# Attention, a mixture of experts and a SoLU layer in one kernel: the tiles of results moved to the front of the freed memory, and expert 1's weights issued ahead of its rows

## The chip, the cores and the metric

The kernel runs on one core of a Trainium2 chip. The metric is the device time of one execution in microseconds (us). A core has five engines with a queue of instructions each: PE (matrix products), DVE and ACT (element by element), POOL, and SP, which here only issues DMA transfers. Each queue runs in its own order, and an instruction that waits holds up all that stand behind it in its queue. A wait is a wait on counters: every engine raises a counter of its own as its instructions end, every DMA queue likewise.

## The reference

```
scores = q @ k^T / 8, times gamma_h**(i-j) for i >= j        # 4 x 8 heads x 576 x 64
x      = (scores @ v) as 2304 rows of 512
e_i    = argmax(x_i @ w_gate);  gate_i = softmax(...)[e_i]    # 8 experts, capacity 576
y_i    = gate_i * (relu(x_i @ w1[e_i]) @ w2[e_i])             # 512 -> 1024 -> 512
h      = y @ w_in;  s = h * softmax(h);  out = layernorm(s) * g @ w_out
```

## The kernel before

Attention runs over 20 chunks of 128 rows, its instructions in an order written out by hand (PERIOD, and DRAIN for the end). Each chunk's rows of x are scattered by expert into a table `xs` in DRAM (L524). Every fp32 operand is split into a high and a low fp16 part, and a product takes three matmuls.

Expert 0's first 192 rows are computed inside attention's last part (steps `el`, `ehm`, `eym`), into `eyh` and `eyl`. DRAIN ends with `cp`, the function `places`: nine small DVE instructions whose last is `offi` (L604), the places where each expert's results go.

Then `expert(e)` runs for e = 0 to 7 in the order of their loads. It takes its rows from `xs` by a transposing DMA into `xT` (`x_load`, 144 rows for what is left of expert 0, 352 for expert 1), makes four hidden pairs (fp = 0 to 3, PE L256 to L258 into `hps`), each read out by ACT (`hh`, L262) and DVE (`hl`, L266), and two output pairs (dp = 0, 1, PE L280 to L282 into `yps`), which ACT and DVE write into the tiles of results `y_hi` and `y_lo` (L286, L290). `hps` and `yps` turn through three buffers of PSUM, so a pair can start when the pair three before it has been read out.

An expert's weights come in eight parts of 512 KB, each loaded by SP into one of four `stage` buffers (`wst`, L204 and L208), split by ACT (`wh`, L178) and then by DVE (`wl`, L181). `w_step` does DVE's half of one part, issues the next load, and then ACT's half of a later part. Parts 1 to 8 are expert 0's and are loaded and split in attention; parts 9 to 16 are expert 1's (9 to 12 for hidden pairs 0 to 3, 13 to 16 for the outputs), and 17 on are expert 2's.

POOL clears the unused part of `y_hi` and `y_lo` (L1110), copies the early results in (L1107, L1108), and writes zeros into rows of `xs` that no token filled (`blank_rows`, L948). `blank_rows(NUT)` and `blank_rows(0)` stand before `x_load(1)`, which reads such rows, and behind `x_load(0)`, which reads the same table.

Memory of a core's partitions is handed out in pools, one behind the other. Attention has the pools `attn` and, behind it, `at_one`; when both are closed, the later pools are laid over them. Bytes in a partition, as the built program places them:

| pool | before | after |
|---|---|---|
| attn (freed) | 90336 to 180864 | the same |
| at_one (freed) | 180864 to 209824 | the same |
| ybuf (y_hi, y_lo) | | 90336 to 130272 |
| f64p (f64raw) | 90336 to 98528 | 130272 to 138464 |
| f3 | 98528 to 114912 | 138464 to 154848 |
| wk (xT, hh, hl, th) | 114912 to 151520 | 154848 to 191456 |
| big | 151520 to 224224 (y_hi, y_lo at its start) | 191456 to 224224 |

Of the kernel before, what the change touches and what calls it, by code (L numbers as in the profile page):

```python
# [10 lines left out]
F32 = mybir.dt.float32  # L11
F16 = mybir.dt.float16
# [8 lines left out]
N = B * S  # L21
DM = H * D
E = 8
# [8 lines left out]
COLS = (336, 352, 328, 312, 304, 296, 288, 280)  # L32

EARLY = 192
# [12 lines left out]
def rows16(n):  # L47

    return -(-n // 16) * 16
# [63 lines left out]
def tile_attention_moe_solu(ctx: ExitStack, tc: tile.TileContext, a: dict, cols, cols16):  # L113
    nc = tc.nc
    act, dve, pool, pe, sp = nc.scalar, nc.vector, nc.gpsimd, nc.tensor, nc.sync
# [97 lines left out]
    def w_load(e, h, part):  # L213
        if e not in number:
            number[e] = sp.value_load(order[0:1, e:e + 1], min_val=1, max_val=E - 1)
        wraw[e, h, part] = w_raw(number[e], h, part)
# [15 lines left out]
    def w_load_next():  # L232
        if nload[0] < len(wsteps):
            w_load(*wsteps[nload[0]])
            nload[0] += 1

    def w_hi_next(limit):
        if nhi[0] < min(limit, len(wsteps)):
            split_hi(*w_parts(*wsteps[nhi[0]]))
            nhi[0] += 1  # L240

    def w_lo_next():

        if nconv[0] < nhi[0]:
            split_lo(*w_parts(*wsteps[nconv[0]]))
            wraw.pop(wsteps[nconv[0]])
            nconv[0] += 1
            return True
# [12 lines left out]
    def hidden_hi(ps, hid, fp, n):  # L261
        act.activation(hid[0][:, 2 * fp:2 * fp + 2, :n], ps[:, :, :n], AF.Relu)  # L262
# [26 lines left out]
    def y_out_lo(ps, n, dst_lo, th):  # L289
        dve.tensor_tensor(dst_lo, ps[:, :, :n], th[:, :, :n], op=ALU.subtract)  # L290
# [237 lines left out]
    early = {}  # L528
# [230 lines left out]
    ps_pools[:] = [psA, psC, psA]  # L759


    f64p = ctx.enter_context(tc.tile_pool(name="f64p", bufs=1))
    f64raw = f64p.tile([128, 2, 512, 2], I32, name="f64raw")
    f3 = ctx.enter_context(tc.tile_pool(name="f3", bufs=2))
    wk = ctx.enter_context(tc.tile_pool(name="wk", bufs=2))
    big = ctx.enter_context(tc.tile_pool(name="big", bufs=1))
    fin = ctx.enter_context(tc.tile_pool(name="fin", bufs=1))
    s3 = ctx.enter_context(tc.tile_pool(name="s3", bufs=5))
    CMAX = max(COLS)
    LAST = [min(N, sum(COLS[:e])) for e in range(E)]  # L770
    YW = max([N] + [n + c for n, c in zip(LAST, COLS)])
    y_hi = big.tile([128, 4, YW], F16, name="y_hi")
    y_lo = big.tile([128, 4, YW], F16, name="y_lo")
    w_in_hi = big.tile([128, 4, F], F16, name="w_in_hi")
    w_in_lo = big.tile([128, 4, F], F16, name="w_in_lo")
    w_out_hi = big.tile([128, 8, DM], F16, name="w_out_hi")
# [168 lines left out]
    def blank_rows(t):  # L945

        n, u = ((E - 1) * (UNIT - 1), 1) if t == NUT else (min(128, (E - 1) * NUNIT - 128 * t), UNIT)
        pool.indirect_dma_start(out=xs_by[NCH + t].rearrange("(u r) w -> u (r w)", r=u),  # L948
                                out_offset=bass.IndirectOffsetOnAxis(ap=blank[0:n, t:t + 1], axis=0),
                                in_=f64raw[:n].rearrange("p i f t -> p (i f t)").bitcast(F16)[:, 0:u * 2 * DM], in_offset=None,  # L950
                                bounds_check=E * NR // u - 1, oob_is_err=False)

    def x_load(e):
        if e:
            n = rows16(COLS[e])
            rows = xs[:].rearrange("(e n) w -> e n w", e=E)[bass.ds(number[e], 1), 0:n, :].rearrange("e n w -> (e n) w")
        else:
            n = COLS[0] - EARLY
            rows = xs[bass.ds(sp.value_load(starti[0:1, 0:1], min_val=0, max_val=EARLY), n), :]
        xT[e] = wk.tile([128, 8, n], F16, tag="xT", name="xT")  # L960
        sp.dma_start_transpose(out=xT[e], in_=rows)
# [20 lines left out]
    def w_step(limit):  # L982

        if w_lo_next():
            w_load_next()
        w_hi_next(limit)
# [13 lines left out]
    def expert(e):  # L1000
        w = [wsplit.pop((e, 0)), wsplit.pop((e, 1)), None, None]
        C = COLS[e] if e else COLS[0] - EARLY
        hid = (wk.tile([128, 8, CMAX], F16, tag="hh", name="hh"), wk.tile([128, 8, CMAX], F16, tag="hl", name="hl"))
        for fp in range(4):
            ps = hidden_mm(w, xT[e], fp, C)
            if e or fp:
                w_step(8 * e + 12)
            hidden_hi(ps, hid, fp, C)
            hidden_lo(ps, hid, fp, C)
            f64_step(e, fp)  # L1010
            if e:
                next(side, None)
            if fp == min(e, 1) and e + 1 < E:
                x_load(e + 1)
                if not e:
                    for t in range(1, NUT):
                        blank_rows(t)
                if not e:
                    w_load_next()
        w[2], w[3] = wsplit.pop((e, 2)), wsplit.pop((e, 3))  # L1020
        at, top = (offi[0:1, e:e + 1], LAST[e]) if e else (starti[0:1, 0:1], EARLY)
        ra = act.value_load(at, min_val=0, max_val=top)
        rv = dve.value_load(at, min_val=0, max_val=top)
        for dp in range(2):
            ps = y_mm(w, hid, dp, C)
            if e:
                for _ in range(2):
                    w_step(8 * e + 16)
            th = wk.tile([128, 2, CMAX], F16, tag="th", name="th")
            y_out_hi(ps, C, y_hi[:, 2 * dp:2 * dp + 2, bass.ds(ra, C)], th)  # L1030
            y_out_lo(ps, C, y_lo[:, 2 * dp:2 * dp + 2, bass.ds(rv, C)], th)
            f64_step(e, 4 + dp)
            if not e:
                for _ in range(2):
                    w_step(8 * e + 16)


    sol = {}
# [59 lines left out]

    inorder = ExitStack()
    inorder.enter_context(tc.manual_schedule())  # L1100
    x_load(0)
    pool.memset(f64raw, 0)
    blank_rows(NUT)
    blank_rows(0)
    for _ in range(3):
        w_load_next()
    pool.tensor_copy(y_hi[:, :, 0:EARLY], early["y"][0])  # L1107
    pool.tensor_copy(y_lo[:, :, 0:EARLY], early["y"][1])  # L1108
    for t in (y_hi, y_lo):
        pool.memset(t[:, :, COLS[0]:N].bitcast(F32), 0.0)  # L1110
    for e in range(E):
        if e == 1:
            f64_next(0)
# [6 lines left out]
    for j in range(NT):  # L1120
        c = slice(128 * j, 128 * j + 128)
# [14 lines left out]
    with tc.For_i(0, nany, 1):  # L1136
        nblk = nc.values_load(bcnt[0:1, 0:1], min_val=0, max_val=NBLK)
        with tc.For_i(0, nblk, 1) as i:
            row = sp.value_load(brow[0:1, bass.ds(i, 1)], min_val=0, max_val=E * NR - 128)
            ex = sp.value_load(bexp[0:1, bass.ds(i, 1)], min_val=0, max_val=E - 1)  # L1140
            xb = wk.tile([128, 8, CMAX], F16, tag="xT", name="xb")
            w = []
# [22 lines left out]
            for h in range(4):  # L1165
                hi = wpool.tile([128, 2048], F16, tag="wh", name="whb")
                lo = wpool.tile([128, 2048], F16, tag="wl", name="wlb")
                for part in range(2):
                    t = w_raw(ex, h, part)
                    cs = slice(1024 * part, 1024 * part + 1024)  # L1170
                    split_weights(hi[:, cs], lo[:, cs], t, WS)
                w.append((hi, lo))
            hid = (wk.tile([128, 8, CMAX], F16, tag="hh", name="hhb"), wk.tile([128, 8, CMAX], F16, tag="hl", name="hlb"))
            for fp in range(4):
                hidden_pair(w, xb, hid, fp, 128)
            for dp in range(2):
                y_pair(w, hid, dp, 128, y_hi[:, 2 * dp:2 * dp + 2, 0:128], y_lo[:, 2 * dp:2 * dp + 2, 0:128],
                       wk.tile([128, 2, CMAX], F16, tag="th", name="th"))
            M_in("b", y_hi[:, :, 0:128], y_lo[:, :, 0:128], mb[:, 0:1])
# [6 lines left out]
        with tc.For_i(0, ndrop, 1):  # L1186

            for ch in range(NCH):
                b, c = divmod(ch, CPB)
                n = csize(ch)  # L1190
# [43 lines left out]
```

## Time and profile before

| | us |
|---|---|
| median of 3 runs | 529.32 (529.21 to 531.28) |
| the profiled execution | 529.27 |
| its span, first to last instruction | 527.4 |
| what lies around the span | 1.87 |

| engine | busy us | share |
|---|---|---|
| PE | 504.9 | 96% |
| DVE | 348.3 | 66% |
| ACT | 278.9 | 53% |
| POOL | 150.8 | 29% |

Attention is over for PE at 135 us, expert 0 runs to 147, expert 1 to 176, the other experts to 324, the SoLU layer to the end. PE's busy time counts overlapping matmuls once, and a matmul's row lasts longer than the distance to the next one, so the starts of the matmuls tell more than their durations.

### The profile page before, as it was taken

The page shows a single profiled execution, that of the slowest core. Times are in us where ns is not written, and L with a number is a line of the kernel's source. Part 1 is how long each engine was busy: PE and PEld are TensorE (multiplying, and loading weights), DVE is VectorE, ACT ScalarE, POOL GpSimd, SP SyncE. Part 2 cuts the span into 40 slices and gives each one's busy share as a digit, 9 for nine tenths or more (in the row PEclk, how much of TensorE's full clock was granted, in tenths as well). Part 3 has the DMA queues.
Part 4 walks back from the last instruction along what each step waited for, and adds up shares of the span by engine and source line. Part 5 has one row for each costly group of instructions (what it writes and reads, how often), then busy time and mean ns, then how long its engine had stood idle before and what let it go on. Part 6 is the DMA issues. An engine that isn't in the chain of part 4 may idle for free.

```text
span 527.4 us, 11770 instructions
## 1 busy us (share of the span) xinstructions
PE 504.9 (96%) x4616; PEld 341.2 (65%) x4616; DVE 348.3 (66%) x839; ACT 278.9 (53%) x452; POOL 150.8 (29%) x183
## 2 busy tenths in 40 slices
PE   8889999999998999999999998999999999999992
PEld 4779999989975677777777786444444444444440
DVE  0478778878657796969889994386565555556520
ACT  4688888873445646465657661264434433443430
POOL 3638687844650000202010000022221231131130
PEclk9999999999999999999999999999999999999997
DMA  8999998222689796968798830037234333333431
GB/s 214 228 248 247 256 284 208 103 62 91 177 265 281 239 257 225 250 212 253 259 238 274 219 121 0 1 64 116 60 81 93 68 80 82 79 76 71 94 81 44
DMA packets 139485, 83.09 MB, mean 158 GB/s; under 512 B 100053, under 2 KB 126581, under 8 KB 139389
## 3 DMA queue, kind: packets, MB, share of 16 engines
q1 hardware_dynamic: 135742, 72.53, 54.5%
q0 software_dynamic: 3680, 9.74, 5.3%
q8 instruction: 38, 0.62, 0.5%
q14 instruction: 25, 0.20, 0.2%
HBM read 57.21 MB, written 15.21 MB: 137 GB/s over the span
## 4 chain that ended last, share of the span: by engine, by line
PE 69%; DMA 10%; DVE 9%; issue 4%; ACT 2%; SPq 2%; POOL 1%; POOLq 0%; DVEq 0%; ACTq 0%
PE hp L1049 6%; PE hp L1048 6%; PE hp L1047 6%; PE op L1087 5%; PE op L1088 5%; PE op L1089 5%; PE yps L282 4%; PE yps L280 4%; PE yps L281 4%; DMA wst<-in_w 4%; PE hps L256 3%; PE hps L258 3%; PE hps L257 3%; PE sc L417 3%; PE xo L437 3%
## 5 line engine op out<-in xcount | busy, mean ns | idle before, releaser
L178 ACT ACTIVATE wh<-wst 128x1024 f16<-128x1024 f32 x64 | 67.1, 1054 | 45.5 <-DMA wst<-in_w 45.1
L181 DVE SCALAR_TENSOR_TENSOR wl<-wst,wh 128x1024 f16<-128x1024 f32 x64 | 77.7, 1231 | 2.9 <-ACT wh L178 1.4
L282 PE MATMUL yps<-hl,wh 128*128 128x144 f16 (+7 forms) x256 | 72.0, 286 | 2.5 <-DVE hl L266 2.5
L256 PE MATMUL hps<-xT,wh 128*128 128x144 f16 (+7 forms) x256 | 72.0, 286 | 2.3 <-DVE hl L266 2.1
L280 PE MATMUL yps<-hh,wh 128*128 128x144 f16 (+7 forms) x256 | 72.0, 286 | 0.5 <-DVE hl L266 0.5
L281 PE MATMUL yps<-hh,wl 128*128 128x144 f16 (+7 forms) x256 | 72.0, 286 | 0.0
L258 PE MATMUL hps<-xT,wl 128*128 128x144 f16 (+7 forms) x256 | 72.0, 286 | 0.0
L257 PE MATMUL hps<-xT,wh 128*128 128x144 f16 (+7 forms) x256 | 72.0, 286 | 0.0
L1062 POOL TENSOR_TENSOR t<-t,c 128x2 f32<-128x2 f32 x18 | 12.7, 705 | 185.4 <-DVE t L1061 185.4
L1087 PE MATMUL op<-w_out_hi,uT 128*128 128x512 f16 x144 | 54.6, 379 | 0.0
L1047 PE MATMUL hp<-w_in_hi,y_hi 128*128 128x512 f16 x144 | 54.6, 379 | 0.0
L1048 PE MATMUL hp<-w_in_lo,y_hi 128*128 128x512 f16 x144 | 54.6, 379 | 0.0
L1088 PE MATMUL op<-w_out_lo,uT 128*128 128x512 f16 x144 | 54.6, 379 | 0.0
L1089 PE MATMUL op<-w_out_hi,uT 128*128 128x512 f16 x144 | 54.6, 379 | 0.0
L1049 PE MATMUL hp<-w_in_hi,y_lo 128*128 128x512 f16 x144 | 54.4, 379 | 0.0
L1055 ACT ACTIVATE ex<-hp,t,ct 128x1024 f32<-128x1024 f32 x18 | 21.7, 1205 | 50.6 <-DVE t L1053 50.6
L870 POOL TENSOR_TENSOR sc<-sc,vals 128x180 bf16<-128x180 bf16 x10 | 8.7, 867 | 104.3 <-DVE sc L838 59.3
L422 DVE TENSOR_TENSOR P<-sc,decay 128x1024 f32<-128x1024 f32 (+1 forms) x20 | 22.3, 1114 | 22.0 <-PE sc L417 22.0
L1057 DVE SCALAR_TENSOR_TENSOR u<-hp,ex 128x1024 f32<-128x1024 f32 x18 | 22.0, 1223 | 21.7 <-ACT ex L1055 21.7
L1060 ACT ACTIVATE jk<-u,t 128x1024 f16<-128x1024 f32 x18 | 20.7, 1148 | 27.9 <-DVE t L1058 21.3
L280 PEld LDWEIGHTS <-wh 128*128 128x128 f16 x288 | 28.2, 98 | 10.4 <-issue 3.1
L257 PEld LDWEIGHTS <-wh 128*128 128x128 f16 x288 | 28.2, 98 | 9.9 <-issue 2.7
(223 smaller groups left out, 1069.2 us busy)
## 6 DMA issues: line engine op xcount, KB each, us to landing
wst<-in_w SPq DMA_DIRECT2D x64, 512.0 KB, 4.9
k<-in_k SPq DMA_DIRECT2D x16, 256.0 KB, 6.0
q<-in_q SPq DMA_DIRECT2D x8, 512.0 KB, 7.1
v<-in_v SPq DMA_DIRECT2D x16, 256.0 KB, 5.8
f64raw<-in_w_in SPq DMA_DIRECT2D x8, 512.0 KB, 4.1
f64raw<-in_w_out SPq DMA_DIRECT2D x8, 512.0 KB, 4.8
xs<-zero SPq DMA_DIRECT2D x1, 672.0 KB
decay<-in_decay SPq DMA_DIRECT2D x1, 512.0 KB, 7.2
```

What stands on the lines that cost most here:

```text
L256: pe.matmul(ps[:, i, :n], lhsT=hi[:, c0:c0 + 128], rhs=x[:, kk, :n], start=(kk == 0), stop=False)
L257: pe.matmul(ps[:, i, :n], lhsT=hi[:, c0:c0 + 128], rhs=x[:, 4 + kk, :n], start=False, stop=False)
L258: pe.matmul(ps[:, i, :n], lhsT=lo[:, c0:c0 + 128], rhs=x[:, kk, :n], start=False, stop=(kk == 3))
L280: pe.matmul(ps[:, i, :n], lhsT=hi[:, c0:c0 + 128], rhs=hh[:, kk, :n], start=(kk == 0), stop=False)
L281: pe.matmul(ps[:, i, :n], lhsT=lo[:, c0:c0 + 128], rhs=hh[:, kk, :n], start=False, stop=False)
L282: pe.matmul(ps[:, i, :n], lhsT=hi[:, c0:c0 + 128], rhs=hl[:, kk, :n], start=False, stop=(kk == 7))
L1047: pe.matmul(hp[:, i], lhsT=yh[:, kk], rhs=w_in_hi[:, kk, c], start=(kk == 0), stop=False)
L1048: pe.matmul(hp[:, i], lhsT=yh[:, kk], rhs=w_in_lo[:, kk, c], start=False, stop=False)
L1049: pe.matmul(hp[:, i], lhsT=yl[:, kk], rhs=w_in_hi[:, kk, c], start=False, stop=(kk == 3))
L1087: pe.matmul(op, lhsT=s["uT"][:, kk], rhs=w_out_hi[:, kk], start=(kk == 0), stop=False)
L1088: pe.matmul(op, lhsT=s["uT"][:, kk], rhs=w_out_lo[:, kk], start=False, stop=False)
L1089: pe.matmul(op, lhsT=s["uT"][:, 8 + kk], rhs=w_out_hi[:, kk], start=False, stop=(kk == 7))
```

## The change

The two tiles of results get a pool of their own, `ybuf`, ahead of `f64p`. At the experts' start SP issues part 9 before `x_load(0)` and parts 10 and 11 behind it; part 12 is issued in expert 0's fp = 0, and `x_load(1)` goes from fp = 0 to fp = 2. POOL clears `y_hi` and copies its early part before the two `blank_rows`, and clears `y_lo` after them. In expert 0 the two `w_step`s of each output pair stand before the pair's read-out instead of behind it.

```diff
+    CMAX = max(COLS)
+    LAST = [min(N, sum(COLS[:e])) for e in range(E)]
+    YW = max([N] + [n + c for n, c in zip(LAST, COLS)])
+    ybuf = ctx.enter_context(tc.tile_pool(name="ybuf", bufs=1))
+    y_hi = ybuf.tile([128, 4, YW], F16, name="y_hi")
+    y_lo = ybuf.tile([128, 4, YW], F16, name="y_lo")
     f64p = ctx.enter_context(tc.tile_pool(name="f64p", bufs=1))
     f64raw = f64p.tile([128, 2, 512, 2], I32, name="f64raw")
...
-    y_hi = big.tile([128, 4, YW], F16, name="y_hi")
-    y_lo = big.tile([128, 4, YW], F16, name="y_lo")
...
             f64_step(e, fp)
             if e:
                 next(side, None)
-            if fp == min(e, 1) and e + 1 < E:
+            if not e and not fp:
+                w_load_next()
+            if fp == (1 if e else 2) and e + 1 < E:
                 x_load(e + 1)
                 if not e:
                     for t in range(1, NUT):
                         blank_rows(t)
-                if not e:
-                    w_load_next()
...
         for dp in range(2):
             ps = y_mm(w, hid, dp, C)
-            if e:
-                for _ in range(2):
-                    w_step(8 * e + 16)
+            for _ in range(2):
+                w_step(8 * e + 16)
             th = wk.tile([128, 2, CMAX], F16, tag="th", name="th")
...
-            if not e:
-                for _ in range(2):
-                    w_step(8 * e + 16)
...
+    w_load_next()
     x_load(0)
+    for _ in range(2):
+        w_load_next()
     pool.memset(f64raw, 0)
+    pool.memset(y_hi[:, :, COLS[0]:N].bitcast(F32), 0.0)
+    pool.tensor_copy(y_hi[:, :, 0:EARLY], early["y"][0])
     blank_rows(NUT)
     blank_rows(0)
-    for _ in range(3):
-        w_load_next()
-    pool.tensor_copy(y_hi[:, :, 0:EARLY], early["y"][0])
+    pool.memset(y_lo[:, :, COLS[0]:N].bitcast(F32), 0.0)
     pool.tensor_copy(y_lo[:, :, 0:EARLY], early["y"][1])
-    for t in (y_hi, y_lo):
-        pool.memset(t[:, :, COLS[0]:N].bitcast(F32), 0.0)
```

SP's queue at the experts' start, before: first the loading of a register for expert 0's rows, then those rows, then three parts of expert 1's weights, then expert 1's rows. In brackets are the counters that an instruction waits for: `X_49` is raised by engine X, `DMASW` by POOL's and `DMAHW` by SP's transfers.

```order
L959 TENSOR_LOAD starti [waits DVE_49]
...
L961 DMA_TRANSPOSE xT<-xs 128x8x144 [waits DMASW3_49,DMASW7_49,DMASW2_49,DMAHW0_49,DMASW1_49,DMAHW5_49,DMASW0_49,DMAHW6_49,DVE_49,DMAHW7_49,Activation_49,Pool_49]
L215 TENSOR_LOAD order [waits DVE_49]
...
L204 DMA wst<-in_w 128x4x256 [waits DMAHW2_49]
L961 ISA
L961 DMA_TRANSPOSE xT<-xs 128x8x352 [waits DMAHW1_49,DMASW5_49,DMASW4_49]
L204 ISA
L204 DMA wst<-in_w 128x4x256 [waits DMAHW3_49]
```

The same place after:

```order
L215 TENSOR_LOAD order [waits DVE_49]
...
L204 DMA wst<-in_w 128x4x256 [waits DMAHW5_49,DVE_49,Activation_49]
L960 TENSOR_LOAD starti
...
L962 DMA_TRANSPOSE xT<-xs 128x8x144 [waits DMASW3_49,DMASW2_49,DMASW7_49,DMASW1_49,DMAHW0_49,DMASW0_49,DMAHW4_49,DVE_49,DMAHW6_49,PE_49,DMAHW7_49,Activation_49,Pool_49]
...
L204 DMA wst<-in_w 128x4x256 [waits DMAHW3_49,DMAHW1_49]
L208 ISA
L208 DMA wst<-in_w 128x2x512 [waits DMAHW5_49,DVE_49,Activation_49]
L962 ISA
L962 DMA_TRANSPOSE xT<-xs 128x8x352 [waits DMASW5_49,DMASW4_49]
```

One part of weights stands before expert 0's rows, and part 12 and part 13 (`128x2x512`) before expert 1's. The transfer of expert 0's rows has PE's counter among its waits, which it had not. Its waits on ACT and DVE were there before, on other counts: in the built program DVE's count was that of chunk 19's L517 and is that of `offi` (L604), ACT's was that of chunk 19's L487 and is that of the last `eth` (L287), and PE's is that of the last L282 inside attention.

DVE's queue from the first instruction of `places` that reads `room` to expert 0's third `hl`, before:

```order
L600 TENSOR_TENSOR m_e<-kept,room 128x8
L266 SCALAR_TENSOR_TENSOR hl<-hps,hh 128x2x144
L566 TENSOR_TENSOR w_2752<-gt,m_e 128x64
L567 TENSOR_REDUCE off<-w_2752 128x8
L566 TENSOR_TENSOR w_2756<-at,off 128x64
L567 TENSOR_REDUCE start_at<-w_2756 128x8
L604 CAST offi<-start_at 128x8
L266 SCALAR_TENSOR_TENSOR hl<-hps,hh 128x2x144
```

The same place after:

```order
L600 TENSOR_TENSOR m_e<-kept,room 128x8
L566 TENSOR_TENSOR w_2752<-gt,m_e 128x64
L567 TENSOR_REDUCE off<-w_2752 128x8
L566 TENSOR_TENSOR w_2756<-at,off 128x64
L567 TENSOR_REDUCE start_at<-w_2756 128x8
L604 CAST offi<-start_at 128x8
L266 SCALAR_TENSOR_TENSOR hl<-hps,hh 128x2x144 x2
```

Expert 0's first `hl` stood inside `places` and now stands behind `offi`. POOL's queue from the clearing of `f64raw`, before:

```order
L948 DMA xs<-f64raw,blank 19456x1024
L948 DMA xs<-f64raw,blank 4864x4096
L1107 COPY y_hi<-eyh 128x4x192
L1108 COPY y_lo<-eyl 128x4x192
L1110 MEMSET y_hi 128x4x984
L1110 MEMSET y_lo 128x4x984
L948 DMA xs<-f64raw,blank 4864x4096 x4
```

The same place after:

```order
L1103 MEMSET y_hi 128x4x984
L1104 COPY y_hi<-eyh 128x4x192
L949 DMA xs<-f64raw,blank 19456x1024
L949 DMA xs<-f64raw,blank 4864x4096
L1107 MEMSET y_lo 128x4x984
L1108 COPY y_lo<-eyl 128x4x192
L949 DMA xs<-f64raw,blank 4864x4096 x4
```

`y_hi` is ready before the blank rows are written, `y_lo` after it.

## Rows read from the trace of the kernel before

**Rows 1.** What PE waited for, in total: us, times, longest us.
```profile
PE yps L282 <- DVE hl L266: 2.5, 3, 1.6
PE hps L256 <- DVE hl L266: 2.1, 1, 2.1
```

**Rows 2.** PE's instructions: start us, us, engine, line, operation [idle before, releaser].
```profile
134.80 0.25 PE L282 MATMUL yps<-ehl,wh 128*128 128x192 f16 x1
135.21 0.22 PE L256 MATMUL hps<-xT,wh 128*128 128x144 f16 x1 [0.17 <-DMA xT<-xs]
...
147.34 0.31 PE L256 MATMUL hps<-xT,wh 128*128 128x352 f16 x1
...
157.93 0.31 PE L258 MATMUL hps<-xT,wl 128*128 128x352 f16 x1
160.33 0.31 PE L256 MATMUL hps<-xT,wh 128*128 128x352 f16 x1 [2.09 <-DVE hl L266]
...
169.54 0.31 PE L281 MATMUL yps<-hh,wl 128*128 128x352 f16 x1
170.32 0.31 PE L282 MATMUL yps<-hl,wh 128*128 128x352 f16 x1 [0.47 <-DVE hl L266]
```

**Rows 3.** The chain of work that ended last, from 131 us: start us, us, what.
```profile
131.68 3.40 DMA xT<-xs
...
137.23 4.98 DMA xs<-f64raw,blank
142.26 2.65 SPq L961
145.11 5.61 DMA wst<-in_w
...
153.09 4.54 DMA wst<-in_w
```

**Rows 4.** SP's DMA issues after expert 0's rows, columns as in rows 2.
```profile
133.80 1.60 SPq L204 DMA_DIRECT2D wst<-in_w  x3
```

**Rows 5.** POOL's instructions, columns as in rows 2.
```profile
136.00 0.93 POOL L948 DMA_INDIRECT xs<-f64raw,blank  x1 [2.44 <-DMA xT<-xs]
...
139.63 0.82 POOL L1107 COPY y_hi<-eyh 128x768 f16<-128x768 f16 x1 [1.43 <-DVE offi L604]
```

**Rows 6.** DVE's instructions, columns as in rows 2.
```profile
129.33 0.17 DVE L589 CAST order<-byrank 128x8 int32<-128x8 f32 x1
...
135.99 0.56 DVE L290 TENSOR_TENSOR eyl<-yps,eth 128x384 f16<-128x384 f32 x1 [2.26 <-ACT eth L287]
...
137.20 0.23 DVE L600 TENSOR_TENSOR m_e<-kept,room 128x8 f32<-128x8 f32 x1
...
138.27 0.21 DVE L566 TENSOR_TENSOR w<-gt,m_e 128x64 f32<-128x64 f32 x1
...
139.28 0.17 DVE L604 CAST offi<-start_at 128x8 int32<-128x8 f32 x1
```

**Rows 7.** PE at the start, columns as in rows 2.
```profile
1.16 4.45 PE L639 MATMUL wps<-zero 128*128 128x512 f16 x10 [1.16 <-DVE zero L642]
...
8.06 1.90 PE L639 MATMUL wps<-zero 128*128 128x512 f16 x8
```

**Rows 8.** The last matmul, columns as in rows 2.
```profile
517.07 0.38 PE L1089 MATMUL op<-w_out_hi,uT 128*128 128x512 f16 x1
```

**Rows 9.** Stretches at the end: length; PE, PEld, DVE, ACT, POOL busy; PEclk; DMA.
```profile
520.00:521.00 1.00, 0.00 (x0) 0.00 (x0) 0.00 (x0) 0.00 (x0) 0.00 (x0) 1.00 0.76 258
521.00:522.00 1.00, 0.00 (x0) 0.00 (x0) 0.00 (x0) 0.00 (x0) 0.00 (x0) 0.72 0.03 12
522.00:523.00 1.00, 0.00 (x0) 0.00 (x0) 0.00 (x0) 0.00 (x0) 0.00 (x0) 0.50 0.06 16
```

**Rows 10.** ACT's late read-outs for experts 0 and 1, columns as in rows 2.
```profile
145.57 0.41 ACT L286 ACTIVATE y_hi<-yps 128x288 f32 x1 [2.97 <-POOL y_hi L1110]
...
158.61 0.74 ACT L262 ACTIVATE hh<-hps 128x704 f16<-128x704 f32 x1
```

More of the change, by code (lines that the diff above doesn't have):

```diff
@@ L768, in tile_attention_moe_solu @@
     s3 = ctx.enter_context(tc.tile_pool(name="s3", bufs=5))
-    CMAX = max(COLS)
-    LAST = [min(N, sum(COLS[:e])) for e in range(E)]
-    YW = max([N] + [n + c for n, c in zip(LAST, COLS)])
-    y_hi = big.tile([128, 4, YW], F16, name="y_hi")
-    y_lo = big.tile([128, 4, YW], F16, name="y_lo")
     w_in_hi = big.tile([128, 4, F], F16, name="w_in_hi")
```

## The prediction

> **What bounds the kernel now.** I read the waits of PE first, since PE is busy for 96% of the span, and there only two waits near the change: 2.1 us for a hidden pair and 2.5 us in three places for outputs, all for DVE's `hl` [rows 1]. PE's own rows put them in time. Expert 1's first matmul starts at 147.34, and its pace is (157.93 - 147.34) / 71 steps = 0.149 us. The start at 160.33 comes 2.40 us behind the one ahead of it, 2.25 more than the pace, and the one at 170.32 comes 0.78 behind, 0.63 more [rows 2]. Together 2.9 us. Expert 0's 192 matmuls run from 135.21 to 147.34 without a hole, 0.063 us each.
>
> Then the chain of waits, to see what makes `hl` late. Expert 0's rows take 3.40 us from 131.68; the blank rows, which must not overwrite what that transfer reads, take 4.98 from 137.23; `x_load(1)` needs them and holds SP until 142.26 + 2.65; only then part 12 is issued, at 145.11, and takes 5.61; its split frees the buffer for part 16, which is loaded in 4.54 from 153.09 [rows 3]. ACT's split of part 16 stands ahead of expert 1's first read-out, which so starts at 158.61 [rows 10], and PE's fourth hidden pair needs the PSUM buffer that this read-out frees. That is the chain that the change cuts.
>
> **The change part by part.** The sum is made against the profiled execution, 529.27 us: the span of 527.4 and 1.87 around it. The median is 529.32, so no correction between them.
>
> 1) *Part 12 ahead of `x_load(1)`.* Part 12 no longer waits for the blank rows; the parts behind `x_load(1)` are now 14 to 16, and part 16 waits for neither part 12 nor its splits. If all of it holds, 2.25 + 0.63 = 2.9 us go. The bounds are 0 and -2.9; I take -2.9, since expert 1's fourth pair comes 3 x 24 x 0.149 = 10.7 us after its first, and part 16, issued some 3 us before that first, has time to land (5.61 at the slowest in the chain [rows 3]) and be split.
>
> 2) *The pools.* This is the part that I think decides. `attn` has 90528 bytes; before, f64p, f3 and wk together take 61184 and lie wholly on it. With `ybuf`'s 39936 in front they end at 191456, and `at_one` starts at 180864: wk now straddles both. A tile of such a pool waits for all that used the memory under the pool, whether or not its own bytes were touched. The trace shows this with the pool that straddled them before, `big`: POOL's copy into `y_hi`, whose bytes lie on `attn` alone, stood idle for 1.43 us until DVE's `offi`, the last of `at_one`'s users [rows 5]. Now the copy is free of it, and wk's first tile inherits it. That tile is `xT` of expert 0, and the order's waits show it: `x_load(0)` waits for PE, and for `offi` on DVE.
>
> When is `offi` done? PE's last early matmul starts at 134.80 [rows 2], ACT follows, DVE's last `eyl` starts at 135.99 and four of the nine instructions of `places` end at 137.20 + 0.23 = 137.43. The other five took from 138.27 to 139.28 + 0.17 = 139.45, which is 1.18; what lay between was expert 0's first `hl`, which now stands behind [rows 6]. So `offi` ends at 137.43 + 1.18 = 138.61. SP starts `x_load(0)` at about 138.7 instead of 131.68 [rows 3], 7.0 us later, and PE's next instruction in order is the first matmul on those rows. It moves from 135.21 to 142.2, and PE has nothing else to do from 134.80 + 0.25 = 135.05 on [rows 2]. Term: +7.0, with little room either way (a contended or an idle DMA: 6.5 to 7.5).
>
> Behind the waiting transfer in SP's queue stand parts 10 to 12. They were issued at 133.80 and in the 1.6 us behind [rows 4]; now they go out from 138.7 + 1.3 to about 141.6 and land by 147.2 at part 12's pace. Their splits belong to expert 0's pairs at 145 to 149, so this costs ACT some waiting but PE nothing. Part 9, ahead of the transfer, needs only `order`, done at 129.33 + 0.17 [rows 6], before SP's old start. POOL's blank rows wait for `x_load(0)` as before, 0.9 us behind its end (135.08 to 136.00 [rows 3, 5]), so they and `x_load(1)` move by the same 7.0, and expert 1's rows stay as far ahead of expert 1 as they were.
>
> 3) *TensorE's clock.* PE now idles for 7.1 us. In this trace it is never without work for that long between the first matmul and the last. After the last, from 517.07 + 0.38 = 517.45 on, the granted clock was 1.00 until 521, 0.72 in the next microsecond's mean and 0.50 after 522, the lower level of 1.2 GHz [rows 8, 9]: it fell while PE had done nothing for less time than the new hole. So I expect expert 0 to start at the lower level. Its price shows at the kernel's start: ten L639 matmuls took 4.45 us there, eight of the same form 1.90 later, 0.42 against 0.22 each without the tail of the last [rows 7]. A burst like the first at half the pace loses half of its 4.24 us (the tail left out), 2.1; if it is slow for as long as from 1.16 to 8.06, 3.4; if the clock stays up, 0. I take 2.1.
>
> The Trainium skill ("TensorE: Matmul & The Clock Gate", "Part 1: The HAM clock gate") says that 1.2 GHz is the state that an idle array falls back to and that activity releases it. By that rule the sum below holds, and without it the sum is 2.1 lower; the rows at this trace's end agree with it.
>
> 4) *`y_hi` and `y_lo` cleared sooner.* ACT's write into `y_hi` had waited 2.97 us for POOL [rows 10], but PE had run on through it (no hole before 160.33 [rows 2]). Nothing to win: 0. `y_hi` is ready before expert 0's outputs exist. `y_lo`'s clearing, behind the blank rows at 143 to 145, ends at some 150, and the first `y_lo` is wanted at 153 or later.
>
> 5) *The `w_step`s ahead of expert 0's read-outs.* ACT now splits parts 12 and 13 before the first read-out, and 14 and 15 before the second, and 14 and 15 are loaded behind `x_load(1)`, at about 152 to 153, landing at 158 to 159 at part 12's pace. So the second read-out ends at about 162, and expert 1's third pair, due at 163.4 with the slow clock, needs its PSUM buffer. Covered by some 1.4 us; if that cover goes, 0 to 2 us come back. I take 0.
>
> Sum: +7.0 + 2.1 - 2.9 = +6.2, so 529.27 + 6.2 = 535.5 us.
>
> **Rivals.**
>
> *The clock stays up.* The transfer's wait is as above, but PE runs at once at 2.4 GHz: 529.27 + 7.0 - 2.9 = 533.4. For it: the fall was seen at one place only. Against it: the hole is about 7.1 us, and at the end the clock fell after less idle time than that [rows 8, 9].
>
> *The stall of expert 1 stays, as a wait for outputs.* The second read-out of expert 0 holds a PSUM buffer until parts 14 and 15 have landed (5 above); with the transfers of expert 1's rows and three parts at once they take longer than 5.6 us, and 2.9 us or as much as that are lost at the third pair. Then 529.27 + 7.0 + 2.1 = 538.4. For it: `x_load(1)` is still ahead of these loads, as it was of part 12. Against it: all of this now stands against a PE that is later by 9.
>
> *The wait ends with PE's last early matmul.* If `xT` is let go at 135.05 and not by `offi`, the transfer starts at 135.1, 3.4 us later than before, with a hole too short to expect a fall of the clock: 529.27 + 3.4 - 2.9 = 529.8. For it: PE is the counter that is new in the wait. Against it: POOL's copy waited for `offi` itself.
>
> *The wait costs nothing, and the change is faster.* If `x_load(0)` starts at 131.68 as before, because the scatter that it also waits for is what ends last, only the gain is left: 529.27 - 2.9 = 526.4. It decides as long as `offi` ends before 131.7; `eyl` alone starts at 135.99, so the trace speaks against it.
>
> **How the numbers follow.** Forecast 0.60, clock up 0.14, stall kept 0.14, the wait ended by PE 0.07, no wait 0.05. A measurement of this kernel tells about 0.5% from no change, 2.6 us, so 526.7 and 531.9 are the borders. Slower are the first three, 0.88; within it the fourth, 0.07; faster the last, 0.05. The range runs from 532.5, which is 0.9 below the case of the clock that stays up and takes in that part of the two later waits for outputs (2.5 - 0.47 us [rows 1, 2]) goes too, to 538.6, just above the kept stall; it leaves out the last two cases and the tail of a longer slow stretch.
>
> **What would show it.** The step on the pools: the start of `x_load(0)` in SP's rows at 138 to 139 and a hole of about 7 us on PE ahead of its first L256 on 144 columns, with DVE's `offi` or the transfer named. The clock: granted clock of 0.50 around 140 and 0.12 us between expert 0's first matmuls. The cut chain: no wait at expert 1's fourth pair. POOL's `y_hi` cleared at 134 to 137, the copy no longer behind `offi`. The forecast is wrong if `x_load(0)` starts before 136, or if expert 1 waits again.

## The result, and the profile after

The changed kernel takes 538.15 us (median of 4 runs, 536.37 to 539.3), the kernel before 529.91 on the same chip; the ratio is 1.0124, 95% interval 1.009 to 1.0158. The change makes the kernel slower by about 1.2%. The forecast was 535.5 with a range of 532.5 to 538.6: right in direction, inside the range, 2.65 us low.

The profiled execution took 537.75 us, its span 536.0 instead of 527.4. The totals of PE's waits after the change (us, times, longest us):

```profile
PE hps L256 <- DMA xT<-xs: 7.7, 1, 7.7
PE yps L282 <- DVE hl L266: 2.5, 3, 1.6
PE yps L280 <- ACT hh L262: 0.9, 1, 0.9
```

The first row is new. The 2.1 us for the hidden pair in [rows 1] is gone, and the outputs have a wait of 0.9 for ACT that they did not have. PE's own rows after the change (start us, us, engine, line, operation [idle before, releaser]) put them in time:

```profile
136.12 0.25 PE L282 MATMUL yps<-ehl,wh 128*128 128x192 f16 x1
144.02 0.28 PE L256 MATMUL hps<-xT,wh 128*128 128x144 f16 x1 [7.65 <-DMA xT<-xs]
...
157.45 0.31 PE L256 MATMUL hps<-xT,wh 128*128 128x352 f16 x1
...
178.18 0.31 PE L280 MATMUL yps<-hh,wh 128*128 128x352 f16 x1 [0.87 <-ACT hh L262]
178.33 0.31 PE L281 MATMUL yps<-hh,wl 128*128 128x352 f16 x1
179.10 0.31 PE L282 MATMUL yps<-hl,wh 128*128 128x352 f16 x1 [0.47 <-DVE hl L266]
```

Against [rows 2], the last early matmul starts at 136.12 instead of 134.80. No edit touches PE's work ahead of it, and in the profiles of this study it starts anywhere from 133.57 to 137.37, so the 1.3 us are chance. I therefore compare what comes behind it, in four pieces: the hole (from the start of the last early matmul to expert 0's first matmul), expert 0 (to expert 1's first matmul), expert 1 (to expert 2's first) and the rest.

| us | hole | expert 0 | expert 1 | rest | sum |
|---|---|---|---|---|---|
| before | 0.41 | 12.13 | 31.63 | 348.4 | 392.6 |
| after | 7.90 | 13.43 | 30.30 | 348.3 | 399.9 |
| difference | +7.49 | +1.30 | -1.33 | -0.2 | +7.3 |

What released expert 0's rows is read from three engines' rows after the change. DVE's end of the attention:

```profile
140.10 0.17 DVE L604 CAST offi<-start_at 128x8 int32<-128x8 f32 x1
```

SP's transfers behind it:

```profile
140.46 1.31 SPq L962 DMA_TRANSPOSE xT<-xs  x1
142.00 1.60 SPq L204 DMA_DIRECT2D wst<-in_w  x3
150.81 0.37 SPq L208 DMA_DIRECT2D wst<-in_w  x1
151.37 3.80 SPq L962 DMA_TRANSPOSE xT<-xs  x1
```

And POOL's copy of the early results:

```profile
138.01 0.82 POOL L1104 COPY y_hi<-eyh 128x768 f16<-128x768 f16 x1
```

`x_load(0)` goes out 0.2 us behind the end of `offi` (140.10 + 0.17), 8.8 us later than in [rows 3]; POOL's copy, which had waited for `offi` in [rows 5], no longer does. The wait has changed its owner. The last SP row shows something else: expert 1's rows stand right behind a load of part 13 (L208, 150.81). In before nothing stood there.

The clock, by stretches (length; PE, PEld, DVE, ACT, POOL busy; PEclk; DMA share; GB/s):

```profile
136.00:140.00 4.00, 0.37 (x5) 0.14 (x2) 2.45 (x9) 0.87 (x2) 2.76 (x2) 1.00 0.00 0
140.00:141.00 1.00, 0.00 (x0) 0.00 (x0) 0.24 (x2) 0.00 (x0) 0.00 (x0) 0.61 0.00 0
141.00:144.00 3.00, 0.00 (x0) 0.01 (x1) 0.00 (x0) 0.00 (x0) 0.00 (x0) 0.50 0.58 128
144.00:147.00 3.00, 2.98 (x26) 3.00 (x27) 0.00 (x0) 0.00 (x0) 1.92 (x3) 0.50 1.04 342
147.00:148.00 1.00, 1.00 (x18) 1.00 (x17) 0.34 (x1) 0.78 (x2) 1.00 (x2) 0.98 1.10 356
```

The granted clock falls to 0.50 inside the hole, and expert 0 runs its first 3.0 us there, at 26 matmuls where full speed has 48.

Last, the chain of waits of the changed kernel from expert 1 on (start us, us, what):

```profile
157.58 0.34 POOL xs L949
...
161.84 7.05 DMA xs<-f64raw,blank
169.02 0.36 SPq L302
...
170.17 6.23 DMA wst<-in_w
176.43 0.29 ACT wh L178
...
177.39 0.75 ACT hh L262
178.16 0.90 DVE hl L266
...
179.10 0.31 PE yps L282
```

POOL's later blank rows (`t` = 1 to 4) wait for expert 1's rows to land, `f64raw`'s two loads (L302) wait for the blank rows, parts 19 and 20 stand behind those on SP, and ACT's split of such a part stands ahead of the last `hh`. This is where the wait of 0.9 us comes from.

Of one kernel below, e6, only the time is used, since the execution that was profiled was a disturbed one.

### The profile page after: what moved, and what is told of

Its sections match the earlier page's. It is cut to its first block, busy times and chain, and to the rows that moved or that the text cites. A ratio compares the mean times of both kernels' runs of the same rounds, so it can differ in the third digit from the quotient of the medians.

```text
span 536.0 us, 11767 instructions
## 1 busy us (share of the span) xinstructions
PE 506.4 (94%) x4616; PEld 342.7 (64%) x4616; DVE 348.4 (65%) x839; ACT 279.4 (52%) x452; POOL 150.5 (28%) x183
## 4 chain that ended last, share of the span: by engine, by line
PE 71%; DMA 8%; DVE 8%; issue 6%; POOL 2%; ACT 2%; SPq 1%; POOLq 0%; DVEq 0%; ACTq 0%
PE hp L1046 6%; PE hp L1045 6%; PE hp L1044 6%; PE yps L282 5%; PE yps L280 5%; PE yps L281 5%; PE op L1084 5%; PE op L1085 5%; PE op L1086 5%; PE hps L256 4%; PE hps L258 4%; PE hps L257 4%; PE sc L417 3%; PE xo L437 3%; PE xo L432 2%
## 5 line engine op out<-in xcount | busy, mean ns | idle before, releaser
L256 PE MATMUL hps<-xT,wh 128*128 128x144 f16 (+7 forms) x256 | 73.2, 289 | 7.7 <-DMA xT<-xs 7.7
L282 PE MATMUL yps<-hl,wh 128*128 128x144 f16 (+7 forms) x256 | 72.0, 286 | 2.5 <-DVE hl L266 2.5
L257 PE MATMUL hps<-xT,wh 128*128 128x144 f16 (+7 forms) x256 | 73.1, 289 | 0.0
L258 PE MATMUL hps<-xT,wl 128*128 128x144 f16 (+7 forms) x256 | 73.1, 289 | 0.0
```

Of the source, the lines that this page charges most:

```text
L256: pe.matmul(ps[:, i, :n], lhsT=hi[:, c0:c0 + 128], rhs=x[:, kk, :n], start=(kk == 0), stop=False)
L257: pe.matmul(ps[:, i, :n], lhsT=hi[:, c0:c0 + 128], rhs=x[:, 4 + kk, :n], start=False, stop=False)
L258: pe.matmul(ps[:, i, :n], lhsT=lo[:, c0:c0 + 128], rhs=x[:, kk, :n], start=False, stop=(kk == 3))
L282: pe.matmul(ps[:, i, :n], lhsT=hi[:, c0:c0 + 128], rhs=hl[:, kk, :n], start=False, stop=(kk == 7))
```

## The experiments

Ratios are to the kernel before, run on the same chip, with 95% intervals. The other columns are those of the table above, from one profile each. Of e6 only the time is given.

| kernel | ratio | hole | expert 0 | expert 1 | sum |
|---|---|---|---|---|---|
| after | 1.0124 (1.0090 to 1.0158) | 7.90 | 13.43 | 30.30 | 399.9 |
| e1 SP's order alone | 0.9987 (0.9963 to 1.0012) | 1.21 | 14.54 | 29.24 | 393.2 |
| e2 pools alone | 1.0084 (1.0054 to 1.0113) | 7.54 | 13.94 | 28.64 | 398.3 |
| e3 `f3` behind `wk` | 1.0008 (0.9983 to 1.0033) | 1.24 | 15.30 | 29.55 | 394.2 |
| e4 hole filled | 1.0132 (1.0092 to 1.0173) | 8.16 | 13.91 | 32.53 | 402.9 |
| e5 part 12 first | 1.0029 (1.0007 to 1.0051) | 0.17 | 15.46 | 30.51 | 394.4 |
| e6 and `f64raw` later | 1.0011 (0.9988 to 1.0034) | | | | |
| e7 mended | 1.0006 (0.9977 to 1.0036) | 1.59 | 12.49 | 30.04 | 392.4 |
| e8 rows at the old step | 1.0099 (1.0080 to 1.0118) | 7.77 | 13.55 | 28.64 | 398.1 |
| e9 the same, filled | 1.0118 (1.0087 to 1.0149) | 8.20 | 13.92 | 33.71 | 404.0 |
| e10 read-out first | 0.9979 (0.9955 to 1.0003) | 0.08 | 12.93 | 29.19 | 391.9 |
| e11 in all experts | 1.0010 (0.9982 to 1.0037) | 0.08 | 12.82 | 28.66 | 391.3 |
| e12 two parts ahead | one run, 532.96 us | 0.09 | 20.49 | 28.64 | 397.3 |

### Which part of the change costs: e1, e2, e3

**e1** is the change without its pools and without POOL's new order. Against after:

```diff
-    y_hi = ybuf.tile([128, 4, YW], F16, name="y_hi")
-    y_lo = ybuf.tile([128, 4, YW], F16, name="y_lo")
...
+    y_hi = big.tile([128, 4, YW], F16, name="y_hi")
+    y_lo = big.tile([128, 4, YW], F16, name="y_lo")
...
```

> The changed kernel with the pools and POOL's order of before: only SP's order and the place of expert 0's w_steps are changed. Theory W (wk's pool reaches into at_one, so xT of expert 0 waits for offi): no hole ahead of expert 0, x_load(0) at about 131.7 us of the span, no wait at expert 1's fourth hidden pair, but the waits at its outputs (0.6 us before, 2.0 after) stay: 527 to 529 us, 1 to 2.5 below before. Theory Q (the part of weights and the register loads put ahead of x_load(0) in SP's queue delay it): the hole of some 7 us stays, 536 to 538 us.

**e2** is the pools alone: before, with `ybuf` first and nothing else.

> The kernel before with the one edit that y_hi and y_lo stand in a pool of their own ahead of f64p; SP's, POOL's and DVE's code as before. W: hole of 7 to 7.5 us ahead of expert 0, the clock falls (1.3 us more), and the waits in expert 1 are those of before or 1 us less, since all its loads move along: 537 to 539.5 us. Q, or a theory M that POOL's clearing of y_hi ahead of the blank rows makes the change slow: no hole, 529 to 531 us.

**e3** is the whole change with two lines exchanged, so that `wk` lies on the attention's first pool alone and `f3`, used much later, straddles:

```diff
-    f3 = ctx.enter_context(tc.tile_pool(name="f3", bufs=2))
...
+    f3 = ctx.enter_context(tc.tile_pool(name="f3", bufs=2))
```

> The changed kernel with the pool f3 made after wk instead of before it, so that wk ends at 175072 and lies on attn alone, and f3, first used in expert 1, straddles. W: no hole; the blank rows go out some 1.7 us later than before, behind the clearing of y_hi and its copy, which makes expert 1's rows late by up to 1.6; expert 1's waits are 1.3 to 2.2 less: 527.5 to 530.5 us. Q or M: the hole stays, 536 to 538 us.

PE's rows of e2 (columns as above):

```profile
135.30 0.25 PE L282 MATMUL yps<-ehl,wh 128*128 128x192 f16 x1
142.84 0.28 PE L256 MATMUL hps<-xT,wh 128*128 128x144 f16 x1 [7.29 <-DMA xT<-xs]
...
156.78 0.31 PE L256 MATMUL hps<-xT,wh 128*128 128x352 f16 x1
```

and of e3:

```profile
135.71 0.25 PE L282 MATMUL yps<-ehl,wh 128*128 128x192 f16 x1
136.95 0.22 PE L256 MATMUL hps<-xT,wh 128*128 128x144 f16 x1 [0.99 <-DMA xT<-xs]
```

The hole of 7 us is there with the pools alone and gone with SP's new order alone; and an exchange of two pool lines takes it out of the whole change, with POOL's new order still in. So it is the pool under expert 0's rows, and neither the order of the loads nor POOL's clearing.

SP's new order has a smaller price of its own. In the five kernels that ask for expert 0's rows first and keep the pools of before (before, e5, e10, e11, e12) the hole is 0.08 to 0.41 us; in the three that have part 9 ahead of those rows and `wk` on `attn` alone (e1, e3, e7) it is 1.21 to 1.59. In before the rows are asked for at 131.68 [rows 3], 0.07 us ahead of POOL's clearing of `f64raw`, which waits for the last scatter into `xs`:

```profile
131.75 1.81 POOL L1102 MEMSET f64raw<- 128x2048 int32 x1 [3.06 <-DMA xs<-row,sloti]
```

In e3 they are asked for 0.91 us behind that clearing, and 1.52 behind part 9:

```profile
132.20 1.81 POOL L1102 MEMSET f64raw<- 128x2048 int32 x1 [2.61 <-DMA xs<-row,sloti]
```

```profile
131.59 0.42 SPq L204 DMA_DIRECT2D wst<-in_w  x1
133.11 1.66 SPq L962 DMA_TRANSPOSE xT<-xs  x1
```

In e1 and e7 they stand as far behind part 9 (1.52 and 1.53), and 0.56 and 0.93 behind the clearing. In the changed kernel the wait for `offi` covers this: `x_load(0)` goes out 0.2 us behind `offi` there, as it does in e2 with the old order.

The runs also held two surprises. In e2, whose loads are in the old order, expert 1 takes 28.64 us, the pace of its matmuls without any wait: the stall of [rows 1] went by itself. Expert 1 starts 9.4 us later than in before (156.78 against 147.34); part 12 goes out 7.8 us later (152.90 against 145.11) but takes 3.9 us to land instead of 5.61, so that it is only 6.1 us later. Expert 1's first read-out starts 8.4 us behind its first matmul (165.14) instead of 11.3 [rows 2, 10]. And e1 and e3, which have neither the hole of 7 us nor the fourth pair's stall, are no faster than before. SP's rows of e1 show where that went:

```profile
144.61 0.37 SPq L208 DMA_DIRECT2D wst<-in_w  x1
145.53 3.83 SPq L961 DMA_TRANSPOSE xT<-xs  x1
```

PE's rows of e1 behind them:

```profile
150.52 0.23 PE L282 MATMUL yps<-hl,wh 128*128 128x144 f16 x1
153.12 0.32 PE L256 MATMUL hps<-xT,wh 128*128 128x352 f16 x1 [2.38 <-DMA xT<-xs]
```

Expert 1's rows, behind part 13, take 7.5 us to land (7.3 in e3) instead of 4.8 in before, and PE waits 2.38 us for them (1.89 in e3). The stall at the fourth pair has become a wait at the first, and the longer hole ahead of expert 0 comes on top.

### What the clock costs: e4, e8, e9

**e4** fills the hole of the changed kernel with 28 matmuls on zeros, in the hand-written order of the attention's tail:

```diff
-            cn eym:0 eyh:0 cu sc:19 eym:1 eyl:0 eyh:1 eyl:1 cp"""
+            cn eym:0 eyh:0 cu sc:19 eym:1 w:28 eyl:0 eyh:1 eyl:1 cp"""
```

> The changed kernel with 28 matmuls on zeros (6.0 us at the upper level) put into the hole, behind the last early matmul. Theory C (the clock falls in the hole and costs expert 0 1.3 us): granted clock 1.00 through expert 0, its 192 matmuls in 12.1 us instead of 13.4, everything else alike: 1.3 us below the changed kernel, 536 to 537 us. If the clock's fall costs nothing, or the fill delays what follows: no difference or slower.

The granted clock stayed at 1.00 through expert 0, and the time did not fall: a miss. Expert 0's own matmuls took 12.1 us again, but PE then waited 1.75 us for expert 1's rows, which landed 7.2 us behind their issue. I took that for part 13's doing, so **e8** asks for the rows two steps sooner, ahead of part 13, and **e9** adds the fill to e8:

```diff
-            if fp == (1 if e else 2) and e + 1 < E:
+            if fp == min(e, 1) and e + 1 < E:
```

> The changed kernel with expert 1's rows asked for two steps earlier (behind part 12, ahead of part 13); the pools stay as in the change, so the hole ahead of expert 0 stays. Theory P (part 13 issued just ahead of the rows made them late, and with them the blank rows, the f64raw loads, parts 19 and 20 and expert 1's outputs): the rows land 4.8 to 5.3 us behind their issue instead of 7.2, the waits at expert 1's outputs go, expert 1 takes 28.6 to 29.3 us instead of 30.3; the hole stays 7 to 7.6 us, expert 0 takes 13.4 us at the lower clock, the end is 398.3 to 399 us behind the last early matmul, ratio 1.008 to 1.010. Rival (the outputs are late for another reason): expert 1 stays at 30.3, ratio 1.0115 to 1.013.

> The same with 28 matmuls on zeros in the hole, as in the earlier kernel that filled it. Theory C (the lower clock costs expert 0 1.3 us, and that was hidden in the earlier run by the late rows of expert 1 alone): granted clock 1.00 throughout, expert 0 takes 12.1 us, expert 1 starts with no wait for xT, and the end is 1.2 to 1.4 us nearer to the last early matmul than in the kernel without the fill, ratio 1.005 to 1.0075, some 0.0025 below the other. Rival (the rows of expert 1 or its weights land at the same time whatever the clock is): expert 1 starts with a wait of about 1 us and the two kernels agree within 0.1%.

e8 came as expected: the rows land in 4.9 us, and expert 1 has no wait and takes 28.64 us, 1.66 less than after. (By time alone its interval still touches that of after.) e9 missed again. Its rows of PE:

```profile
142.10 0.22 PE L256 MATMUL hps<-xT,wh 128*128 128x144 f16 x1 [1.91 <-DMA xT<-xs]
...
156.02 0.32 PE L256 MATMUL hps<-xT,wh 128*128 128x352 f16 x1 [1.76 <-DMA xT<-xs]
...
178.85 0.31 PE L280 MATMUL yps<-hh,wh 128*128 128x352 f16 x1 [2.95 <-ACT hh L262]
```

At full clock expert 0 is done at 154.3, the rows come at 156.0, and the outputs of expert 1 wait 2.95 us behind the same chain of blank rows, `f64raw` and part 19 that the changed kernel showed. And neither fill kept the clock up to the end. It fell again in expert 1, behind the waits for its outputs, in e4 (columns as above):

```profile
178.00:179.00 1.00, 0.86 (x5) 0.56 (x5) 0.86 (x6) 0.11 (x1) 0.00 (x0) 0.80 0.88 206
179.00:182.00 3.00, 3.00 (x12) 1.53 (x11) 2.45 (x3) 0.91 (x1) 0.00 (x0) 0.50 0.90 344
```

and in e9:

```profile
180.00:182.00 2.00, 2.00 (x8) 1.06 (x7) 1.39 (x5) 0.00 (x0) 0.00 (x0) 0.50 0.98 277
```

So the 1.3 us of the slow clock are real in expert 0, and filling the hole took nothing off the time: from e8's 1.0099 a gain of 1.3 us would lead to about 1.0074, below e9's interval (with e8's own interval the two can just touch). Why the gain didn't come is not shown. In these two profiles later transfers and a second slow stretch ate it; but e9's profile (539.72 us) is the second longest of its six runs, and the four that took 535.5 to 536.5 us, which are no faster than e8's median of 535.37 either, have no trace. Why the same rows landed in 4.9 us in e8 and 6.6 in e9, with no weights right ahead in either, I can't say.

### Is the moved part worth anything: e5, e6, e7, e12

**e5** moves part 12 alone, in the kernel before:

```diff
+                if not e:
+                    w_load_next()
                 x_load(e + 1)
...
-                if not e:
-                    w_load_next()
```

> The kernel before with one edit: the load of weight part 12 (512 KB) is issued ahead of expert 1's rows instead of behind them; pools, POOL's order and all else stay as before. Theory H (the stall in expert 1's fourth hidden pair is the late part 12, as the prediction's first step had it): the wait of 2.25 us there goes, expert 1 takes 29.0 to 29.4 us instead of 31.6, the end is 392.6 - 2.3 to 2.9 = 389.7 to 390.3 us behind the start of the last early output matmul, ratio 0.9945 to 0.996. Rival L (512 KB of weights issued just ahead of rows slow their landing, as part 13 did in three runs, 4.8 to 7.3 us): expert 1's rows land 2 us or more later, expert 1 begins with a wait of about 2 us for xT and the ratio is 0.999 to 1.001. H holds the better chance, since part 12 is free to go out right behind parts 9 to 11, some 6 us ahead of the rows.

The chain of e5 (start us, us, what), up to expert 1's first matmul:

```profile
130.22 3.38 DMA xT<-xs
...
135.76 6.68 DMA xs<-f64raw,blank
142.50 6.65 DMA xT<-xs
149.20 0.32 PE hps L256
```

and two of its stretches (columns as above):

```profile
148.00:149.00 1.00, 0.00 (x0) 0.00 (x0) 1.00 (x2) 0.00 (x0) 0.00 (x0) 1.00 1.13 266
...
151.00:153.00 2.00, 2.00 (x9) 1.01 (x8) 0.95 (x2) 1.97 (x4) 1.39 (x3) 0.50 1.01 346
```

H is false as a statement on the time. The fourth pair's stall is gone, but the chain is 19.0 us long from `x_load(0)` to expert 1's first matmul, against 15.7 in before (131.68 to 147.34): the blank rows took 6.68 us instead of 4.98 [rows 3], the rows behind them 6.65 instead of 4.8. PE waited 2.91 us, and on top the clock was at 0.50 for three microseconds *after* the wait. The rival has the place right and the reason wrong: part 12 did not stand right ahead of the rows (it was out by 134.6), it stood ahead of the blank rows.

**e12** looks at that alone: parts 9 and 10 ahead of the blank rows, 11 and 12 behind expert 1's rows.

```diff
                     w_load_next()
+                    w_load_next()
...
-    for _ in range(3):
+    for _ in range(2):
         w_load_next()
```

> The kernel before with two parts of weights (9 and 10) issued ahead of the blank rows instead of three; part 11 goes out with part 12 behind expert 1's rows. A look at the chain of DMAs only. Theory B (each 512 KB ahead of the second set of blank rows costs its landing about 1.7 us): the blank rows land 3 to 4 us behind their issue (4.98 with three parts ahead, 6.68 with four), and expert 1's rows are issued 1 to 2 us earlier in the chain; the stall in expert 1 grows, since part 11 is late: 530 to 535 us. Rival (the landing of the blank rows does not depend on the weights ahead): 4.8 to 5.2 us again.

SP's rows of e12, the two parts and expert 1's rows:

```profile
132.11 1.03 SPq L204 DMA_DIRECT2D wst<-in_w  x2
139.12 2.88 SPq L961 DMA_TRANSPOSE xT<-xs  x1
```

and POOL's second blank rows:

```profile
135.54 0.98 POOL L948 DMA_INDIRECT xs<-f64raw,blank  x1 [0.30 <-issue]
```

The second blank rows, issued at 135.54, let expert 1's rows go at 139.12. From the one issue to the other it is 3.58 us with two parts ahead, 5.03 with three (before; 4.4 to 5.3 in e2 and e7 to e11), 6.74 with four (e5). That is as theory B had it, with one profile each for two and four parts. From the first of these parts' issue to the rows' issue it is 7.0, 8.5 and 10.2 us. (Expert 0's 20.49 us come from part 11, which is late here: PE waited 5.23 us at the outputs, and the clock stood at 0.50 behind the wait.)

**e6** is e5 with `f64raw`'s loads moved behind expert 2's rows.

> As the kernel with part 12 ahead, and the two loads of f64raw are issued behind expert 2's rows instead of ahead of expert 1's weights. Theory F (the two f64raw loads wait for POOL's blank rows, and parts 19 and 20 are queued behind them on SP, so expert 1's split weights and its outputs come late): the waits at expert 1's outputs (0.4 to 0.6 us) go, parts 19 and 20 go out without a wait for the blank rows, expert 1 takes 28.5 to 28.8 us, ratio 0.0005 to 0.001 below the other kernel's, so 0.9935 to 0.995. Rival (the outputs wait for ACT and DVE, which do the hidden's split and the parts' split one after the other): the waits stay and the two kernels agree within 0.1%; or f64raw is late for its own reader and the ratio rises.

It ties with before and with e5; the gain that F asked for isn't there by time, and what the outputs waited for isn't known. **e7** is the changed kernel with `wk` made ahead of `f3`, the blank rows ahead of the clearing of `y_hi`, and expert 1's rows at their old step.

> The changed kernel with three things put back: the pool f3 is made behind wk, so that expert 0's rows wait for nothing in the attention's memory; POOL issues the blank rows ahead of clearing y_hi; expert 1's rows go out behind part 12 and ahead of part 13. Theory B (expert 1's start hangs on a chain of DMAs, expert 0's rows, two sets of blank rows, expert 1's rows, and 512 KB of weights ahead of the blank rows makes that chain longer by about what the fourth pair's stall gave back): no hole, expert 1 starts with a wait for xT of 1.5 to 3 us, no wait at the fourth pair, end 392.5 to 395 us behind the last early matmul, ratio 0.999 to 1.002. Rival (it was part 13 alone that made the rows late in the earlier kernels): no wait at expert 1's start, end 390 to 391, ratio 0.994 to 0.996.

Its ratio is what theory B gives, and its wait isn't: expert 1's first matmul, at 149.57, waited for nothing, and 0.5 us went at the outputs and 0.4 at the third pair. Only parts 10 to 12 lie between the two row transfers here, since part 9 is out before them, and from the one to the other it is 10.64 us, as in before (10.58). What e7 wins in expert 1 it loses ahead of it: the hole is 1.59 us, the price of SP's order as in e1 and e3.

### A version that beats both? e10, e11

The stall of [rows 2] begins where ACT stands in part 16's split with the read-out behind it [rows 10]. **e10** moves no transfer and turns that order round in expert 1; **e11** does so in experts 1 to 7.

```diff
-            if e or fp:
+            if e != 1 and (e or fp):
                 w_step(8 * e + 12)
             hidden_hi(ps, hid, fp, C)
             hidden_lo(ps, hid, fp, C)
+            if e == 1:
+                w_step(8 * e + 12)
```

> The kernel before with one edit and no transfer moved: in expert 1, ACT and DVE read each hidden pair out ahead of the step of the weights' split instead of behind it. Theory A (the stall at the fourth hidden pair is ACT standing in the split of a part that has not landed, with the read-out of the first hidden pair queued behind it): ACT reads the first pair out at about 156 us of the span instead of 158.6, the fourth pair's wait falls from 2.09 us to 0.5 or less, expert 1 takes 29.3 to 29.9 us instead of 31.6, the end is 390.5 to 391 us behind the last early output matmul, ratio 0.9955 to 0.997. Rival G (given back: the splits come 0.7 to 1.6 us later, and with them the weights of the outputs, whose waits grow from 0.6 to 2 us or more): expert 1 stays at 31 us and the ratio is 0.999 to 1.001.

> The same order in experts 1 to 7. No wait of TensorE was seen in experts 2 to 7 of the kernel before, so theory A expects the same time as the kernel with expert 1 alone, within 0.1%. Rival G2 (the splits that come later make the later experts wait for weights): 1 us or more slower than that kernel, seen as new waits of TensorE behind expert 2's start.

ACT's first read-out of expert 1 in e10:

```profile
155.69 0.74 ACT L262 ACTIVATE hh<-hps 128x704 f16<-128x704 f32 x1
```

and the longest wait of PE in its expert 2:

```profile
187.65 0.30 PE L256 MATMUL hps<-xT,wh 128*128 128x328 f16 x1 [0.77 <-DVE hl L266]
```

The first read-out starts at 155.69 as A expected (158.61 before), the fourth pair waits no more, and expert 1 takes 29.19 us, 2.4 less. But 1.3 us come back in expert 2, with waits for DVE that before did not have: G was right on the size of what is given back, wrong on the place. The ratio, 0.9979, has an interval that ends at 1.0003, so a gain isn't established, and e11 has none. No version was found that beats the kernel before.

## Why the prediction was right, point by point

1. *Part 12 ahead (-2.9).* The wait that it named went, but this is the step that failed as a term: expert 1 gained 1.33 us. Two things were missed. The rows of expert 1 were taken to keep their lead; in before they had none (their 4.8 us from 142.26 end at 147.06, expert 1 starts at 147.34), and in the changed kernel they go out behind part 13, which costs expert 1 1.66 us (e8 against after, one profile each). By the prediction's own last sign, "if expert 1 waits again", this step failed: the outputs wait 0.87 us for ACT. And in a kernel that is 7 us late the old order of loads has no stall either (e2), so the moved part gained nothing that the hole did not give without it: alone it made the kernel no faster (e5, e1). Part 9 ahead of `x_load(0)` was put at nothing, since it needs only `order`; without the pools' wait it makes the hole about 1 us longer (e1, e3, e7).
2. *The pools (+7.0).* Right in mechanism and size: 7.49 measured. `offi` ended 4.15 us behind the last early matmul's start, where the prediction had 3.81. That POOL's copy and `x_load(0)` would exchange their waits is what the rows show, and e1 to e3 show the cause.
3. *The clock (+2.1).* It fell as forecast, from 140 on, and expert 0 ran slow for 3.0 us: 1.30 us, the term was too large. Its price was taken from the pace of the kernel's first matmuls, where the trace's granted clock reads 1.00 (1 to 6 us), so the pace alone stood for the lower level. What the fall costs the end stays open: filling the hole gained nothing, but the clock then fell later (e4, e9).
4. *`y_hi` cleared sooner (0)* and 5. *the `w_step`s ahead of the read-outs (0)*: no wait of PE at either place, as said.

The sum of the terms was +6.2; behind the last early matmul 7.3 were measured, and 1.3 more came from an attention that ended later in that execution. That the sum came so near is luck in part: the pools' term was 0.5 too small and the gain of part 12 was put 1.6 too high, while the clock's term was 0.8 too large. Of the rivals, "the clock stays up" has fallen with the clock's rows, "the stall stays" with the missing wait at the third pair, and the two that let the rows go sooner with the 140.46 in SP's rows. What held the forecast up was the one term that was much larger than all others.

## What to carry to other kernels

When a buffer is moved to the front of a memory that an earlier stage leaves, look at which *pool* then lies across two older ones: its first tile waits for the last user of both, and if that tile is the input of the engine that bounds the kernel, the wait is a hole. A stall that is found in the profile is worth its length only if the next limit is further off: follow the transfers beside it (here rows, blank rows, rows, blank rows, `f64raw`, weights) to see how much lead they have before a load is put ahead of them, and how long that load holds the queue that issues them. A kernel that has been delayed at one place can lose its stalls elsewhere, as e2 did, so the terms of such a sum need not add. And a fill that keeps the clock up at one place says little until the clock has been read at the next wait.

## What was not expected of the hardware

- The clock can fall behind a wait, when work has begun again: in e5 TensorE stood from 146.3 to 149.2, the granted clock was still 1.00 in 148 to 149, 0.91 in the microsecond in which work began again, and 0.50 in 151 to 153 with TensorE busy. Expert 1 took 30.51 us there without another wait, 1.9 more than in e2 or e8. The length of the wait alone does not tell: waits of 2.1 to 2.4 us (before, e1) left the clock at 1.00, and in e4 it fell behind waits of 1.42 and 0.47 us (that end at 177.22 and 178.14). What else decides stays open.
- One transfer, expert 1's rows, took from 4.8 to 7.5 us to land. With part 13 right ahead of it 7.2 to 7.5 in e1, e3 and e4 and 6.0 in after; without, 4.8 to 5.2 in before, e2 and e8, yet 6.6 in e5 and e9. The load ahead is part of it; the rest stays open.
- In two kernels DVE stood still while POOL cleared a tile. DVE's `offi` takes 0.17 us in eleven of the thirteen kernels with a profile here. In e3 it takes 3.52 and ends at 144.12, as POOL's clearing of `y_lo` does (140.69 to 144.09); in e7 it takes 2.37 and ends at 143.50, with the clearing of `y_hi` (to 143.46). The `hl`s behind it end then too, and expert 0's first output matmul waited 1.09 us for them in e3 and 0.34 in e7. In before, an `hl` at 143.22, inside a clearing, took its usual 0.44 us, so the clearing alone is not enough; the cause stays open. The row of e3:

```profile
140.60 3.52 DVE L604 CAST offi<-start_at 128x8 int32<-128x8 f32 x1
```
